# Pooled attention's transposes, its place in the order and the staging's margin: three settings of a fused attention and MLP kernel

## The chip, the cores and the metric

The kernel runs as one program on one core of a Trainium2 chip. The metric is the device time of one execution in microseconds (us). Before the change the median of three timed runs is 923.7 us (923.35 to 924.69).

## What is computed

The reference takes q, k and v of shape (4 batches, 8 heads, 576 tokens, 64). It adds two attentions: one on q, k and v averaged over groups of four tokens (144 pooled tokens, the result repeated four times), and one local attention in which a token sees only tokens less than four away. The sum, 2304 tokens by 512, goes through two feed-forward blocks.

```python
out = np.repeat(sm_attn(q_d, k_d, v_d), 4, axis=2) + local_attn(q, k, v)
x = (x @ w_a) * (x @ w_b) @ w_out          # 512 -> 1536 -> 512
h = x @ w_in                               # 512 -> 2048
out = (h * clip(h + 3, 0, 6) / 6) @ w2_out # 2048 -> 512
```

## The kernel before, in words

**Stages.** Weights arrive as 64-bit words and are decoded on ScalarE (ACT) and VectorE (DVE) into 32-bit values (`decode`, from L246 on). Matmuls of the feed-forward blocks run as three passes over a high and a low part of each operand. Tokens are cut into six blocks of 384. Phase 1 multiplies blocks 0 to 2 with `w_a` and `w_b` (12 column tiles f each); phase 2 does the same for blocks 3 to 5. One *job* (`job`) is one block times one f: two products of 12 matmuls (L625) into two PSUM banks; ACT copies the first (L631), DVE multiplies it by the second (L634), and SP stores it. Then follow `w_out` (L729), `w_in` (L876) and the last product (L1015), each in a scheme that works on sums and differences of weight tiles.

**Attention** runs between the jobs. For each batch there are four *groups* (`pooled`, a pair of heads twice over) and five *units* of up to 116 tokens (`local`). A group does: sums of four tokens on DVE (L385, `dqk`), scores on PE (L395, `dsc`), maximum (L400) on DVE, exponentials on ACT (L409), inverse and scaling on DVE (L415, L416, L337), two transposes on PE (`turn`, L427, four 72x72 matmuls each into a PSUM bank of its own), an ACT copy of each into a `deT` tile (`turned`, L434), the product with v (`pv`, L445) and a copy into `od` (L451). A unit does: scores (L496), mask (L504), maximum (L511, L512), exponentials (L521), inverse and scaling (L527, L528, L337), a transpose (L537), its copy (L541), the product with v (L552), the sum with the pooled result (L565, `xf`) and the split of it into the high part (L573, ACT) and the low part (L578, DVE) of the block's `x`. The jobs of a block read all of its `x`; four batches of 576 tokens make six blocks, so batch 2 fills block 3 with units 0 to 3, and its unit 4 and batch 3's units 0 and 1 fill block 4.

From batch 2 on, the product with v of one item and the scores of the item two further on are one PE step (`both`). The next batch's q and k go into the same four `qk` buffers, and are loaded after the last unit's scores of the batch before have been computed.

**Staging.** 22 tiles of the later weights (6 of `wo`, 8 of `w2i`, 8 of `w2o`) are decoded during phases 1 and 2, combined (L1170 on DVE, L1173 on ACT) and written back to HBM (`staged`). Their decode takes the one `dm` buffer: ACT makes the magnitude (L263), DVE does L277, L278 and L282, ACT L271, then DVE L289.

**What sets the order.** The program's order on every engine is worked out when the kernel is built. A planner (`Plan`) keeps a list of steps, each with an engine, a busy time, a `want` (a priority number, not a time; lowest first), what it follows, and tags that it takes and gives back (`BUFS` and the caps below it say how many of each there are). It walks through modelled time, and gives each free engine the ready step of the lowest want whose tags can be had. A step counts as done for those behind it only after its busy time plus a latency of its engine plus `slack`. On the chip each engine then runs its steps in that fixed order and waits on semaphores. The tag `turn` stands for a transpose on its way to ACT's copy; pooled groups and units share it. `pv` (1) and `m` (3) are such tags for products with v and for jobs; all three also take one of four `b` banks.

Jobs follow each other by 384/332 = 1.157 in want. Batch 2's first unit has t = 25.23; its groups have t - 0.05 + 0.01 g. The job before them has wants 24.29 and 24.79 for its two products, the one before that 23.13 and 23.63. Batch 3's first unit has t = 32.26; batch 2's units 3 and 4 have 28.83 and 31.06. Staged tile i has want 3.6 + 2.4 i. While the queue of PE is short of work before the first job, it is given dummy matmuls (L193, `unread`).

Of the kernel before, what the change touches and what calls it, by code (L numbers as in the profile page):

```python
# [29 lines left out]
HP = 4  # L30
# [8 lines left out]
SOON = 14  # L39
# [116 lines left out]
def fused_kernel(ctx: ExitStack, tc: tile.TileContext, qk, vt, vd, wab, wo, w2i, w2o, mask, out):  # L156
# [4 lines left out]
    F1 = wab.shape[0]  # L161
# [28 lines left out]
    def fill():  # L190
        if not unread:
# [4 lines left out]

    plan = Plan()

    BUFS = {"wh": F1, "raw": 3, "dm": 1, "qk": 4, "vraw": 1, "dqk": 2, "de": 2, "dv": 2, "deT": 2, "od": 2, "e": 2,
            "eT": 2, "xf": 2, "x": 3, "a": 3, "b": 4, "s2": 2, "h0": 3, "X": 6, "y": 8, "w2": 2, "q": 8, "x0": 4, "L": 24,  # L200
            "c": 14}
    plan.cap.update(BUFS)

    plan.cap.update({"turn": 1, "pv": 1, "m": 3})
    plan.loose |= {"dm", "b", "turn", "pv", "m", "s2", "e", "de", "eT", "deT", "xf", "dqk", "a", "q", "y", "c"}

    def slot(pool, shape, dtype, tag, name):
        return pool.tile(shape, dtype, tag=tag, bufs=BUFS[tag], name=name)


    def dve(n):
        return 0.07 + 0.00106 * n

    def dve2(n):
        return 0.1 + 0.00055 * n

    def act(n):
        return 0.1 + 0.00095 * n
# [9 lines left out]
    def ACT(busy, want, run, after=(), take=(), give=(), slack=0.0):  # L228
        return plan.add("ACT", busy, want, run, after, take, give, ACT_L + slack)

    def DVE(busy, want, run, after=(), take=(), give=(), slack=0.0):
        return plan.add("DVE", busy, want, run, after, take, give, DVE_L + slack)
# [3 lines left out]
    def DMA(kb, want, run, after=(), take=(), give=()):  # L236
        i = plan.add("SP", dma(kb), want, run, after, take)
        j = plan.add("-", 0, want, lambda: None, [i], give=give, late=DMA_L)
        issued[j] = i
        return j  # L240
# [5 lines left out]
    def decode(src, want, put, tag, after=(), ahead=4, slack=1.0, raw=None, step=CUT, early=False):  # L246

        T = {}

        def load(a, b):  # L250
            def run():
                if a == 0:
                    T["raw"] = slot(xp if raw == "x" else dp, [P, CUT, W // CUT], mybir.dt.uint64, raw or "raw", "raw")
                nc.sync.dma_start(T["raw"][:, a:b], src[a:b].rearrange("a p c -> p a c"))
            return run

        def words():
            w = T["raw"].rearrange("p a c -> p (a c)").bitcast(U32).rearrange("p (n t) -> p n t", t=2)
            return w[:, :, 0], w[:, :, 1]

        def magnitude():
            T["m"] = slot(dp, [P, W], F32, "dm", "m")
            nc.scalar.activation(T["m"], words()[1].bitcast(F32), AF.Abs)  # L263

        def rounded():

            lo = words()[0]
            if early:
                nc.vector.tensor_scalar(lo, lo, 2.0 ** -29, None, op0=ALU.mult)
            else:  # L270
                nc.scalar.activation(lo, lo, AF.Copy, scale=2.0 ** -29)  # L271

        def exponent():
            m = T["m"]
            mu = m.bitcast(U32)

            nc.vector.tensor_scalar(m, m, W_MIN, W_MAX, op0=ALU.max, op1=ALU.min)  # L277
            nc.vector.tensor_scalar(mu, mu, 3, 0x3FFFFFF8, op0=ALU.logical_shift_left, op1=ALU.bitwise_and)  # L278

        def upper():  # L280
            mu = T["m"].bitcast(U32)
            nc.vector.scalar_tensor_tensor(out=mu, in0=words()[1], scalar=0xC0000000, in1=mu,  # L282
                                           op0=ALU.bitwise_and, op1=ALU.bitwise_or)

        def both():

            lo, hi = words()
            mu = T["m"].bitcast(U32)
            nc.vector.tensor_tensor(mu if put is None else hi, mu, lo, op=ALU.add)  # L289

        def first():
            T["w"] = put()
            nc.scalar.activation(T["w"][:, 0], words()[1].bitcast(F32), AF.Copy)

        def second():
            nc.vector.tensor_tensor(T["w"][:, 1], words()[1].bitcast(F32), T["w"][:, 0], op=ALU.subtract)


        i, loads = None, []
        for a in range(0, CUT, step):  # L300
            i = DMA(256 * step, want - ahead, load(a, a + step), [i and issued[i]], take=[] if a else [raw or "raw"])
            loads.append(i)
        i = loads
        j = ACT(act(W), want, magnitude, i, take=["dm"], slack=slack)
        r = DVE(dve2(W), want, rounded, i) if early else ACT(act(W), want, rounded, i, slack=slack)
        i = DVE(2 * dve2(W), want, exponent, [j])
        i = DVE(dve(W), want, upper, [i])
        i = DVE(dve(W), want, both, [i, r], give=[] if put is None else ["dm"], slack=slack)
        if put is None:
            return i, T  # L310
        i = ACT(act(W), want, first, [i, *after], take=[tag], slack=slack)
        return DVE(dve(W), want, second, [i], give=[raw or "raw"])
# [3 lines left out]
    def unit_tokens(u):  # L316
        return min(UT, S - u % NU * UT)
# [5 lines left out]
    for u in range(B * NU):  # L323
        segs[u], off = [], 0
        while off < unit_tokens(u):
            m, at = divmod(at_token, XT)
# [764 lines left out]
    items = []  # L1091
    for u in segs:
        m = segs[u][0][0]
        i = (segs[u][0][1] + UT - 1) // UT
        t = when[m, 0] - 4 + 0.1 * i if m < 3 else when[m - 3, F1 - 1] - 6 + 1.2 * i
        b = u // NU
        if u % NU == 0:
            items.append([pooled(b, g, t - 0.05 + 0.01 * g, b < 1) for g in range(HP)])
        items[b].append(local(u, t, u < 8 and unit_tokens(u) == UT))

    def alone(part):
        busy, want, run, after, take, give = part
        return PE(busy, want, run, after() if callable(after) else after, take, give)

    def both(one, two):
        def run():
            one[2]()
            two[2]()
        return PE(one[0] + two[0] - 0.33, one[1], run, (one[3]() if callable(one[3]) else one[3]) + two[3], one[4] + two[4], one[5] + two[5])
# [7 lines left out]
    for b, batch in enumerate(items):  # L1117
        behind = []
        for item in batch:
            part = next(item)  # L1120
            if len(behind) < (2 if b >= JOIN else 1):
                i = alone(part)
            elif b >= JOIN:
                before, end = behind.pop(0)
                i = both(end, part)
                close(before, i)
            else:
                before, end = behind.pop(0)
                close(before, alone(end))
                i = alone(part)  # L1130
# [7 lines left out]
    i = plan.add("PE", 0.01, -1000, fill, take=["b", "m"])  # L1138
# [11 lines left out]

    def staged(src, want, dest, right):

        i, T = decode(src, want, None, None, step=1, ahead=4 - SOON)

        def v(n):
            return T["m"].rearrange("p (a c) -> p a c", a=CUT)[:, n]

        def t(n):
            return r7()[:, 3 + n]

        def r7():
            return T["raw"].rearrange("p a c -> p (a c)").bitcast(F32).rearrange("p (a c) -> p a c", c=Q)[:, :7]

        def sums():
            if right:
                ops = ((0, v, 3, v, 0), (1, v, 2, t, 0), (2, v, 2, v, 3), (3, v, 1, t, 1))
            else:
                ops = ((0, v, 3, v, 2), (1, t, 0, v, 0), (2, v, 0, v, 3), (3, v, 1, t, 1))
            for k, (to, f, x, g, y) in enumerate(ops):
                nc.vector.tensor_tensor(t(to), f(x), g(y), op=ALU.subtract if right or k else ALU.add)  # L1170

        def copy():
            nc.scalar.activation(r7()[:, 0:3], T["m"].rearrange("p (a c) -> p a c", a=CUT)[:, 0:3], AF.Copy)  # L1173

        j = ACT(act(3 * Q), want, copy, [i])
        k = DVE(4 * dve(Q), want, sums, [i], slack=0.3)
        plan.add("-", 0, want, lambda: None, [j, k], give=["dm"])
        return [DMA(896, want, lambda: nc.sync.dma_start(dest, r7()), [j, k], give=["raw"])]
# [8 lines left out]
    for i, (name, k) in enumerate(S_["staged"]):  # L1187
        src, dest = {"wo_d": (wo, lambda: wo_d[:, :, k]), "wi_d": (w2i, lambda: wi_d[:, 7 * k:7 * k + 7]),
                     "w_d": (w2o, lambda: w_d[k // CUT][:, :, k % CUT])}[name]
        S_[name, k] = staged(src[k], T1 - LEAD - SOON + PACE * i, dest(), name == "w_d")  # L1190
# [164 lines left out]
```

## Time and profile before

| what | us |
|---|---|
| median of the timed runs | 923.7 |
| the profiled execution's own time | 924.78 |
| its span, first to last instruction | 923.0 |
| PE busy in the span | 909.5 |
| DVE busy | 733.5 |
| ACT busy | 537.1 |

PE is TensorE's matmuls, PEld its weight loads, SP the engine that issues most DMAs. "Busy" adds up instruction spans; "[2.88 <-ACT x L573]" behind an instruction says that its engine was idle for 2.88 us just before it, and that the last thing it waited for was ACT's instruction at line 573 that writes `x`. PEclk is the granted TensorE clock as a share of 2.4 GHz, so 0.50 is the level of 1.2 GHz.

### The profile page before, as it was taken

The numbers are of one execution on the slowest core, as the hardware profiler recorded it, in microseconds if no ns is written. First come the engines' busy times: TensorE is split into PE (matmuls) and PEld (weight loads), VectorE is DVE, ScalarE is ACT, GpSimd is POOL, SyncE is SP. The second block draws the span as 40 slices with busy tenths as digits, with TensorE's granted clock in tenths as the row PEclk, the third lists the DMA queues.
The fourth block names the chain that finished last, engine by engine and source line by source line (L and its number), as shares of the span: only waits on it lengthen the run. The fifth ranks groups of instructions, "written<-read, shape, count | busy, mean of one in ns | idle before, by whom it ended". The sixth has DMA issues, their size and how long they took to land.

```text
span 923.0 us, 18730 instructions
## 1 busy us (share of the span) xinstructions
PE 909.5 (99%) x7076; PEld 876.7 (95%) x7076; DVE 733.5 (79%) x1299; ACT 537.1 (58%) x1234; POOL 3.2 (0%) x40
## 2 busy tenths in 40 slices
PE   9999999999989999999999999999999999999998
PEld 6678899999979999999999999999999999999998
DVE  4999987788978987476977798786566899896983
ACT  3778754547656764452745466666566774554551
POOL 0000000000000000000000000000000000000000
PEclk9999999999989999999999999999999999999999
DMA  9645877566765668888454664634348772707301
GB/s 304 229 131 155 287 229 242 189 211 227 274 238 186 212 207 257 269 265 273 138 167 138 191 190 143 206 112 163 137 172 271 252 242 92 251 2 229 114 18 52
DMA packets 121994, 176.91 MB, mean 192 GB/s; under 512 B 9392, under 2 KB 95664, under 8 KB 121904
## 3 DMA queue, kind: packets, MB, share of 16 engines
q1 hardware_dynamic: 121184, 174.49, 57.4%
q8 instruction: 55, 0.90, 0.4%
q10 hardware_dynamic: 720, 1.23, 0.4%
q14 instruction: 35, 0.29, 0.1%
HBM read 113.03 MB, written 62.65 MB: 190 GB/s over the span
## 4 chain that ended last, share of the span: by engine, by line
PE 92%; DVE 5%; DMA 1%; issue 0%; ACT 0%; POOL 0%; SPq 0%; POOLq 0%; ACTq 0%; DVEq 0%
PE pab L625 32%; PE ph L876 19%; PE oacc L1015 19%; PE acc L729 14%; PE po L552 2%; DMA qk<-qk 1%; PE dsc L395 1%; PE dpo L445 1%; PE oacc L1000 1%; PE sc L496 1%; PE dpt L427 1%; PE unread L193 1%; DVE m L282 1%; DVE dqk L385 1%; PE pt L537 1%; DVE mx L511 0%
## 5 line engine op out<-in xcount | busy, mean ns | idle before, releaser
L625 PE MATMUL pab<-x,wh 128*128 128x384 f32 (+2 forms) x1776 | 323.9, 339 | 3.7 <-ACT x L573 2.9
L625 PEld LDWEIGHTS pab<-x,wh 128*128 128x128 f32 x1776 | 305.2, 190 | 7.3 <-ACT x L573 3.0
L876 PE MATMUL ph<-in,wt 128*128 128x384 f32 x1008 | 175.4, 335 | 0.0
L876 PEld LDWEIGHTS ph<-in,wt 128*128 128x128 f32 x1008 | 175.2, 188 | 0.0
L1015 PE MATMUL oacc<-w2o,in 128*128 128x256 f32 x1440 | 172.4, 283 | 0.0
L1015 PEld LDWEIGHTS oacc<-w2o,in 128*128 128x128 f32 x1440 | 172.4, 191 | 0.0
L729 PE MATMUL acc<-hx,wt 128*128 128x384 f32 x756 | 131.2, 334 | 0.0
L729 PEld LDWEIGHTS acc<-hx,wt 128*128 128x128 f32 x756 | 131.1, 188 | 0.0
L631 ACT ACTIVATE a<-pab 128x384 f32<-128x384 f32 (+2 forms) x74 | 35.6, 482 | 97.3 <-PE pab L625 97.2
L634 DVE TENSOR_TENSOR a<-a,pab 128x384 f32<-128x384 f32 (+2 forms) x74 | 40.0, 541 | 54.6 <-PE pab L625 20.0
L680 ACT ACTIVATE hx<-hr 128x768 fp32r<-128x768 f32 x63 | 52.1, 844 | 40.9 <-PE acc L729 22.3
L683 DVE TENSOR_TENSOR hx<-hr,hx 128x768 fp32r<-128x768 f32 x63 | 58.7, 954 | 18.4 <-ACT hx L680 18.1
L803 ACT ACTIVATE in<-gr 128x384 fp32r<-128x384 f32 x96 | 47.2, 520 | 41.7 <-PE oacc L1015 30.9
L893 DVE TENSOR_TENSOR part<-ph,part 128x384 f32<-128x384 f32 x72 | 39.8, 555 | 31.1 <-PE ph L876 19.9
L901 ACT ACTIVATE r<-part,three 128x384 f32<-128x384 f32 x72 | 43.9, 614 | 26.7 <-DVE part L893 25.7
L806 DVE TENSOR_TENSOR in<-gr,in 128x384 fp32r<-128x384 f32 x96 | 49.6, 550 | 8.1 <-ACT in L803 7.3
L803 ACT ACTIVATE in<-e 128x384 fp32r<-128x384 f32 x72 | 37.3, 525 | 28.8 <-PE oacc L1015 23.7
L885 ACT ACTIVATE part<-ph 128x384 f32<-128x384 f32 x72 | 35.1, 490 | 25.0 <-PE ph L876 24.7
L282 DVE SCALAR_TENSOR_TENSOR m<-raw,m 128x1024 uint32<-128x1024 uint32 x34 | 41.5, 1220 | 0.5
L263 ACT ACTIVATE m<-raw 128x1024 f32<-128x1024 f32 x34 | 38.8, 1141 | 4.0 <-DVE raw L1170 2.0
L904 DVE SCALAR_TENSOR_TENSOR r<-r,part 128x384 f32<-128x384 f32 x72 | 38.9, 549 | 0.9 <-ACT r L901 0.9
L806 DVE TENSOR_TENSOR in<-e,in 128x384 fp32r<-128x384 f32 x72 | 37.8, 551 | 0.8 <-ACT in L803 0.5
(95 smaller groups left out, 1036.6 us busy)
## 6 DMA issues: line engine op xcount, KB each, us to landing
g_d<-r SPq DMA_DIRECT2D x96, 192.0 KB, 2.0
gr<-g_d SPq DMA_DIRECT2D x48, 384.0 KB, 4.2
hr<-h_d SPq DMA_DIRECT2D x72, 192.0 KB, 3.7
h_d<-a SPq DMA_DIRECT2D x70, 192.0 KB, 2.4
raw<-wab SPq DMA_DIRECT2D x12, 1024.0 KB, 8.3
raw<-w2i SPq DMA_DIRECT2D x32, 256.0 KB, 4.0
raw<-w2o SPq DMA_DIRECT2D x32, 256.0 KB, 3.4
wi_d<-raw SPq DMA_DIRECT2D x8, 896.0 KB, 4.4
```

The lines of the kernel that those rows point to most:

```text
L282: nc.vector.scalar_tensor_tensor(out=mu, in0=words()[1], scalar=0xC0000000, in1=mu, op0=ALU.bitwise_and, op1=ALU.bitwise_or)
L625: nc.tensor.matmul(T[k], wab_t[f][:, x, c], xs[n][:, g, y, ja:jb], start=(g == 0 and i == 0), stop=(g == KC - 1 and i == 2))
L634: nc.vector.tensor_tensor(T["a"], T["a"], T[1], op=ALU.mult)
L680: nc.scalar.activation(X[n, kk][:, :, 0], src(), AF.Copy)
L683: nc.vector.tensor_tensor(X[n, kk][:, :, 1], src(), X[n, kk][:, :, 0], op=ALU.subtract)
L729: nc.tensor.matmul(acc[n][e], t[:, x, e * P:(e + 1) * P], X[n, kk][:, j, y], start=(kk == 0 and j == 0 and i == 0 and not onto), stop=(kk ...
L803: nc.scalar.activation(x[0][:, 0], src(), AF.Copy)
L806: nc.vector.tensor_tensor(x[0][:, 1], src(), x[0][:, 0], op=ALU.subtract)
L876: nc.tensor.matmul(acc[k], t[:, x, g * P:(g + 1) * P], X[k, g][0][:, y], start=(g == 0 and n == 0 and not onto), stop=(g == 1 and n == 2), ...
L893: nc.vector.tensor_tensor(s[name], acc[k], s[other], op=ALU.add)
L901: nc.scalar.activation(T["r"], src(), AF.Relu, bias=three)
L1015: nc.tensor.matmul(acc[n][e], X[n, k][0][:, x, e * P:(e + 1) * P], t[:, y], start=(k == 0 and i == 0), stop=(k == K - 1 and i == 2))
```

## The change

Four settings are changed. `deT`, the tiles for transposed pooled weights, go from two to four. The tag `turn` goes from one to two. The groups of batches 2 and 3 get a want 1.5 below their first unit's instead of 0.05; with it move the wants of their loads of q, k (6 below) and v, and of all their steps. The decode inside `staged` is planned with slack 0.0 on the steps that had 1.0 (the magnitude L263, the scaling L271, and L289).

```diff
-    BUFS = {... "dv": 2, "deT": 2, "od": 2, "e": 2,
+    BUFS = {... "dv": 2, "deT": 4, "od": 2, "e": 2,
...
-    plan.cap.update({"turn": 1, "pv": 1, "m": 3})
+    plan.cap.update({"turn": 2, "pv": 1, "m": 3})
...
-            items.append([pooled(b, g, t - 0.05 + 0.01 * g, b < 1) for g in range(HP)])
+            items.append([pooled(b, g, t - (1.5 if b > 1 else 0.05) + 0.01 * g, b < 1) for g in range(HP)])
...
-        i, T = decode(src, want, None, None, step=1, ahead=4 - SOON)
+        i, T = decode(src, want, None, None, step=1, ahead=4 - SOON, slack=0.0)
```

## Rows read from the trace of the kernel before

**Rows 1.** The page: busy time of each engine and its share of the span.

```profile
PE 909.5 (99%) x7076; PEld 876.7 (95%) x7076; DVE 733.5 (79%) x1299; ACT 537.1 (58%) x1234; POOL 3.2 (0%) x40
```

**Rows 2.** Stretches: us, busy (count) of PE, PEld, DVE, ACT, POOL; PEclk, DMA, GB/s.

```profile
20.00:62.50 42.50, 39.36 (x574) 28.94 (x571) 40.99 (x75) 31.91 (x133) 0.00 (x0) 1.00 0.65 215
62.50:124.00 61.50, 60.24 (x689) 53.32 (x686) 59.37 (x107) 46.73 (x154) 0.64 (x8) 1.00 0.66 210
240.00:260.00 20.00, 16.22 (x172) 14.86 (x172) 18.93 (x36) 13.13 (x46) 0.64 (x8) 0.94 0.94 319
260.00:900.00 640.00, 640.00 (x4439) 634.83 (x4439) 505.66 (x890) 370.13 (x723) 0.00 (x0) 1.00 0.56 182
```

**Rows 3.** Who PE waited for: us in total, times, longest.

```profile
PE pab L625 <- ACT x L573: 2.9, 1, 2.9
...
PE pab L625 <- DVE x L578: 0.7, 2, 0.4
```

**Rows 4.** Stretches of 2 us about the long stall.

```profile
256.00:258.00 2.00, 0.43 (x1) 0.28 (x1) 2.00 (x3) 1.72 (x9) 0.00 (x0) 0.87 0.97 318
258.00:260.00 2.00, 1.69 (x5) 1.44 (x5) 1.97 (x6) 2.00 (x10) 0.00 (x0) 0.50 1.05 407
...
264.00:266.00 2.00, 2.00 (x13) 2.00 (x12) 0.48 (x2) 0.00 (x0) 0.00 (x0) 0.93 0.19 75
```

**Rows 5.** The chain that ended last, in order of time: start, us, what.

```profile
124.06 53.20 PE pab L625 x300
...
184.14 6.56 PE pab L625 x36
...
255.38 1.23 DVE m L282
256.61 0.55 DVE xf L565
...
258.56 8.95 PE pab L625 x35
```

**Rows 6.** Timeline of PE, batch 2: start, us, line, tiles, count.

```profile
177.09 0.42 PE L427 MATMUL dpt<-ident,de 72*72 72x72 f32 x4
...
195.39 0.71 PE L445 MATMUL dpo<-deT,dv 72*64 72x144 f32 x8
...
198.89 0.41 PE L427 MATMUL dpt<-ident,de 72*72 72x72 f32 x4
199.10 2.36 PE L625 MATMUL pab<-x,wh 128*128 128x384 f32 x12
201.31 0.41 PE L427 MATMUL dpt<-ident,de 72*72 72x72 f32 x4
...
251.71 0.60 PE L537 MATMUL pt<-ident,e 128*128 128x128 f32 x4
252.91 0.71 PE L395 MATMUL dsc<-dqk 64*72 64x144 f32 x8 [0.59 <-DVE dqk L385]
253.55 1.14 PE L552 MATMUL po<-eT,vz 64*64 64x58 f32 x32
```

**Rows 7.** Timeline of DVE: scaling of batch 2's group 0, and of group 2.

```profile
114.89 0.75 DVE L337 TENSOR_TENSOR de<-de,dz 72x576 f32<-72x576 f32 x1
...
192.14 0.76 DVE L337 TENSOR_TENSOR de<-de,dz 72x576 f32<-72x576 f32 x1
```

**Rows 8.** Line 434 on ACT, the copy of a transpose: duration min/median/max in ns.

```profile
L434 ACT ACTIVATE deT<-dpt x32: 382/406/464, 15.4 to 300.0; 72x288 f32<-72x288 f32 x32
```

**Rows 9.** Stretches: all engines, then tile m's instructions on DVE and ACT.

```profile
204.00:262.00 58.00, 54.22 (x564) 51.25 (x561) 51.62 (x104) 39.61 (x125) 0.64 (x8) 0.96 0.74 253
...
204.00:262.00 58.00, 26.54 (x40) 9.88 (x10) 0.96 0.74 253
```

**Rows 10.** Line 277 on DVE waiting for line 263 on ACT: total, times, longest.

```profile
DVE m L277 <- ACT m L263: 2.9, 3, 1.6
```

**Rows 11.** Line 625 alone, from the stall to unit 1 of batch 3.

```profile
257.50:318.20 60.70, 49.54 (x240) 43.96 (x240) 0.94 0.59 211
```

More of the change, by code (lines that the diff above doesn't have):

```diff
@@ L197, in fused_kernel @@
     plan = Plan()
-    BUFS = {"wh": F1, "raw": 3, "dm": 1, "qk": 4, "vraw": 1, "dqk": 2, "de": 2, "dv": 2, "deT": 2, "od": 2, "e": 2,
+    BUFS = {"wh": F1, "raw": 3, "dm": 1, "qk": 4, "vraw": 1, "dqk": 2, "de": 2, "dv": 2, "deT": 4, "od": 2, "e": 2,
             "eT": 2, "xf": 2, "x": 3, "a": 3, "b": 4, "s2": 2, "h0": 3, "X": 6, "y": 8, "w2": 2, "q": 8, "x0": 4, "L": 24,
```

## The prediction

> **What bounds the kernel now.** I read the page first: PE is busy for 909.5 of 923.0 us [rows 1]. The change takes no matmul of the work away and adds none, so nearly all it can win is PE's 13.5 us without work, and slow clock. The windows say where these are. PE is short by 3.1 us from 20 to 62.5 us, where DVE is busy for 40.99 of 42.50; by 1.3 us from 62.5 to 124; by 3.8 us from 240 to 260; and by nothing in the 640 us from 260 to 900 [rows 2]. The rest lies ahead of 20 us and behind 900. The largest gap is thus one place in batch 2's attention. PE's list of waits names it: 2.88 us for the high part of x (L573), 0.3 of the 0.7 us for its low part (L578), and 0.59 us for the sums of batch 3's first group, 3.8 us together [rows 3, 6]. Phase 1's last job is over by then, and block 3's first job needs the x of batch 2's unit 3.
>
> The gap has a second price. The granted clock falls to half at its end and comes back in the window from 264 us [rows 4]. The 35 matmuls behind the gap took 8.95 us; 36 took 6.56 at full clock, so 35 take 6.38, and 2.6 us were lost [rows 5]. Together 6.4 us. (Upper bound for the idle part: from 251.71 to 258.56, 6.85 us, PE had a transpose, scores, a product with v and one matmul of the job to do, 0.60, 0.71, 1.14 and about 0.18 us, so 4.2 us were lost there, and 6.8 in all; the lower figure uses the rows of idle alone, and I take it, as restarts between small matmuls will stay [rows 5, 6].)
>
> The Trainium skill, page "TensorE: Matmul & The Clock Gate", section Terms, prices such a fall as the throttled time times one minus the granted share. By the windows' clocks (0.87, 0.50, 0.50, 0.50 and 0.93 of 2 us each) that is 3.4 us, an estimate by that page, and the time forecast below would be 0.8 us lower; the matmuls' own count decides here.
>
> **Part 1: groups 1.5 earlier.** Group 0 of batch 2 was scaled at 114.89, and its transpose ran at 177.09 [rows 6, 7]: for 62 us it waited for nothing but its want. So a lower want does start the chain sooner. By how much: want 25.18 lies behind the job with 24.29 and 24.79; want 23.73 lies behind the one with 23.13 and 23.63. That is one whole job, 24 matmuls at 53.20/300 us = 4.3 us [rows 5]. (Taken as a rate, 1.5/1.157 jobs, it would be 5.5 us.) The chain's products, exponentials and DVE steps keep their numbers. Of what is moved with them, the loads of q and k of batch 3 do not move by want: their buffers come free with unit 4's scores, so they come earlier only as the units do. The loads of v, issued by SP one job sooner, pass at most the staging's loads; these have three raw buffers, and no row has PE waiting for them. In return one job runs behind the chain instead of ahead of it, at no cost for PE.
>
> **Part 2: two transposes at once, four deT.** Now a group's two transposes, at 198.89 and 201.31, have 12 matmuls between them [rows 6]. With two turns both go together, and that product drops out of each group's chain: 2.4 us by its row. Group 2 was scaled by 192.90 but transposed at 198.89: it waited until group 1's product (195.39) gave back its two deT tiles [rows 6, 7]. With four it needs not, worth up to 6 us more for the units that follow. Along the four groups that is 2.4 us at the least (the other hops hidden behind DVE) and four times that, 9.6 us, at the most. I take 5, between the one hop and the 6 us of the one wait for deT that a row shows. The second turn holds a second of the four banks for about a copy's length; two banks are left for the products when pv has none. A job alternates between two, so no PE wait is booked; if the cover goes, it is at most one ACT copy, 0.41 us, for each of the 12 groups past batch 0, 5 us [rows 8]; no row has PE waiting for a bank.
>
> **Part 3: staging without slack.** No staged tile is waited for by PE in the trace, so finishing it sooner wins nothing. What it can do is take DVE away. In 204 to 262, tile m's instructions hold DVE for 26.54 us, and DVE is busy for 51.62 of 58 [rows 9]: five tiles at 5.3 us. Being far behind its want, staging outranks attention on DVE. Cost, from below: nothing (the waits are where they are). From above: L277 stood up to 1.6 us for L263 [rows 10], so five tiles stand 8.0 us; and if two of some 11.6 us (58/5) for a tile go, 58/9.6 makes six tiles, one more of 5.3 us. I take 2 us, near the lower end, since L277's three waits were 2.9 us in all, and DVE has 6.4 us to spare in the stretch.
>
> **The sum.** Unit 3's low x came at 258.56 and would have to come 4.2 us earlier for PE not to wait. The chain gains 4.3 + 5 and gives back 2: 7.3 us, enough with 3.1 to spare. So the gap goes: 924.78 - 6.4 = 918.4 for an execution like the profiled one. That stood 1.1 us above the median, so against the median 923.7 - 6.4 = **917.3 us**. Nothing is booked for the first 124 us, where DVE sets the pace; the idle time there is kept for the range.
>
> **What is late next.** Block 4 needs batch 3's unit 1. From the gap to that unit's product PE ran 240 of the 288 matmuls (12 jobs) of block 3 [rows 11]; 48 are left, 8.5 us at 0.177. Batch 3's qk loads come sooner with unit 4's scores and its groups gain by part 2 too, so this cover holds or grows.
>
> **Rivals.**
> *The gap shrinks but stays.* The chain gains only 4.3 + 2.4 and loses 4 on DVE, 2.7 of 4.2: about 1.5 us of idle stays, and the clock holds. 923.7 - 2.3 - 2.6 = 918.8. For it: DVE, which every step of the units passes, is 89% busy there [rows 9].
> *The change doesn't do what it says.* The groups start sooner, but DVE works the units off at the same times, as they are late for it and not for PE; same gap, 923.7, within 1.2. Against it: group 2's wait for deT is no DVE wait.
> *Slower: staging takes DVE.* Place: units 0 to 3 of batch 2. Extra DVE time by the upper bounds is 8.0 + 5.3 = 13.3 us; against the chain's least gain of 6.7 the x of unit 3 comes 6.6 us later, 930.3 us. It decides from the point at which DVE loses more than 6.7 + 1.9 us; 927 in its middle. For it: DVE runs in its fixed order, and the 1.23 us of staging just ahead of xf show whom it lets pass [rows 5]. Against it: 6.4 us of spare DVE time [rows 9]. The Trainium skill ("TensorE: Matmul & The Clock Gate", section on the array's architecture) says that ACT and DVE are strictly first in, first out, which is what this rival needs; the trace agrees so far as the 1.6 us of L277 stand with other work behind it.
>
> **How the numbers follow.** The forecast has 0.60, the shrunk gap 0.10, no effect 0.14, slower 0.16. About 0.2%, 1.9 us, can be told from no change. Faster by more is the forecast and the shrunk gap, 0.70; within it 0.14; slower 0.16. Range: down to 914.0 (6.8 for 6.4, the 1.3 us of idle from 62.5 to 124, and 1.6, half of the 3.1 ahead of it), up to 924.0, which takes in no effect and leaves the slower case out. The likeliest case's own range is 914.0 to 919.
>
> **What would show it.** Right: no wait of PE for x L573 or L578 at block 3's first job; PEclk 1.00 from 240 to 280; L427 in rows of x8; batch 2's first L427 about 4 us before 177; first job of phase 2 about 4 us sooner than 257.57. Part 3 wrong: longer waits of L277 for L263, DVE over 95% in that stretch. The forecast fails if PE has a gap of over 2 us anywhere behind 124 us, or PE waits for L631 or L634, a bank.

## The result and the profile after

The changed kernel takes 912.39 us (median of 4 runs, 911.03 to 913.82) beside 923.83 us for the kernel before: a ratio of 0.9875 [0.9858, 0.9892], 11.4 us less. The forecast was 917.3 us with a range of 914.0 to 924.0, so the sign was right and the gain nearly twice the one forecast, outside the range. The execution profiled below took 913.82 us with a span of 912.0; the one before took 924.78 with 923.0. The difference of the spans, 11.0 us, is what follows.

The page of the changed kernel, busy time of each engine (answers to [rows 1]):

```profile
PE 903.5 (99%) x7058; PEld 872.9 (96%) x7058; DVE 732.5 (80%) x1299; ACT 534.4 (59%) x1234; POOL 3.2 (0%) x40
```

PE has 18 instructions fewer. They are the dummies of L193, 36 where there were 54. Its stretches (columns as in [rows 2]):

```profile
20.00:62.50 42.50, 41.03 (x661) 32.38 (x659) 40.24 (x78) 32.79 (x144) 0.00 (x0) 1.00 0.62 202
62.50:124.00 61.50, 61.50 (x628) 55.96 (x627) 57.96 (x99) 44.24 (x138) 0.64 (x8) 1.00 0.62 205
204.00:262.00 58.00, 57.06 (x543) 53.67 (x542) 53.03 (x107) 37.46 (x121) 0.64 (x8) 1.00 0.80 272
240.00:260.00 20.00, 19.40 (x153) 17.36 (x151) 17.12 (x33) 10.30 (x43) 0.00 (x0) 1.00 0.79 261
260.00:900.00 640.00, 639.17 (x4451) 634.48 (x4451) 506.67 (x893) 369.64 (x710) 0.00 (x0) 1.00 0.56 182
```

PE lost 3.8 us from 204 to 262 before [rows 9] and loses 0.94 now, and the granted clock is 1.00 there. From 20 to 124 us it lost 4.4 [rows 2] and loses 1.47. Who PE waited for (columns as in [rows 3]), and its timeline in batch 2 (as in [rows 6]):

```profile
PE unread L193 <- POOL qk L355: 1.9, 1, 1.9
PE pab L625 <- DVE x L578: 1.2, 2, 1.1
PE acc L729 <- DVE a L634: 0.7, 1, 0.7
PE pab L625 <- ACT x L573: 0.4, 1, 0.4
```

```profile
176.52 0.67 PE L427 MATMUL dpt<-ident,de 72*72 72x72 f32 x8
...
188.88 0.67 PE L427 MATMUL dpt<-ident,de 72*72 72x72 f32 x8
...
197.75 0.71 PE L445 MATMUL dpo<-deT,dv 72*64 72x144 f32 x8
...
246.82 0.44 PE L625 MATMUL pab<-x,wh 128*128 128x384 f32 x1 [0.43 <-ACT x L573]
247.43 2.19 PE L625 MATMUL pab<-x,wh 128*128 128x384 f32 x11 [0.17 <-DVE x L578]
```

The 2.88 us for L573 are 0.43. The transposes go in eights. The last product with v (L445) comes at 197.75, 21.2 us behind the first transpose; before it came at 214.31, 37.2 us behind one at 177.09 [rows 6]. Block 3's first job runs on at 247.43 instead of 258.56 [rows 5], 11.1 us sooner: already the whole gain, and only part of it is the gap.

The rest is from before 124 us. The job's matmuls (L625) alone, up to that time, in the kernel before and in the changed one (us, PE busy and count, PEld busy and count, PEclk, DMA, GB/s):

```profile
0.00:124.00 124.00, 47.33 (x277) 42.30 (x277) 1.00 0.70 225
```

```profile
0.00:124.00 124.00, 53.34 (x318) 49.64 (x319) 1.00 0.67 217
```

41 matmuls more are done, 7.2 us of PE at about 0.175 us each, of which 0.6 goes back, as the kernel before had done one more piece of scores by then. So **6.5 us of lead** stand beside **2.8 us of idle time** at the gap, **2.6 us of slow clock** (the prediction's count from [rows 5]; the fall of [rows 4] is gone), and about 1.1 us from transposes that run as eight in 0.67 instead of twice four in 0.41, in the eight groups of batches 2 and 3. Together 13.0 us. The last matmul of a job comes 12.6 us sooner (419.49 for 432.09): the two pitches told in the last section give 1.0 us and take 1.7. From there on 1.6 us go again, 0.71 of them in the new wait at L729's start, and the span is 11.0 shorter.

### The profile page after: what moved, and what is told of

It reads as the page before. It is cut to its first block, busy times and chain, and to the rows that moved or that the text cites. A ratio compares the mean times of both kernels' runs of the same rounds, so it can differ in the third digit from the quotient of the medians.

```text
span 912.0 us, 18711 instructions
## 1 busy us (share of the span) xinstructions
PE 903.5 (99%) x7058; PEld 872.9 (96%) x7058; DVE 732.5 (80%) x1299; ACT 534.4 (59%) x1234; POOL 3.2 (0%) x40
## 4 chain that ended last, share of the span: by engine, by line
PE 88%; DVE 9%; DMA 1%; issue 1%; ACT 0%; POOL 0%; SPq 0%; DVEq 0%; POOLq 0%
PE pab L625 29%; PE ph L876 19%; PE oacc L1015 18%; PE acc L729 14%; PE dsc L395 2%; PE po L552 1%; PE dpo L445 1%; PE oacc L1000 1%; PE unread L193 1%; DVE raw L1170 1%; DVE m L282 1%; PE sc L496 1%; PE dpt L427 1%; DVE dqk L385 1%; DVE m L289 1%
## 5 line engine op out<-in xcount | busy, mean ns | idle before, releaser
L625 PE MATMUL pab<-x,wh 128*128 128x384 f32 (+2 forms) x1776 | 318.2, 337 | 1.7 <-DVE x L578 1.2
L625 PEld LDWEIGHTS pab<-x,wh 128*128 128x128 f32 x1776 | 303.2, 188 | 4.9 <-DVE x L578 1.8
L729 PE MATMUL acc<-hx,wt 128*128 128x384 f32 x756 | 131.3, 334 | 0.7 <-DVE a L634 0.7
L729 PEld LDWEIGHTS acc<-hx,wt 128*128 128x128 f32 x756 | 131.0, 188 | 1.0 <-DVE a L634 1.0
L631 ACT ACTIVATE a<-pab 128x384 f32<-128x384 f32 (+2 forms) x74 | 35.6, 481 | 79.8 <-PE pab L625 78.4
L634 DVE TENSOR_TENSOR a<-a,pab 128x384 f32<-128x384 f32 (+2 forms) x74 | 39.8, 538 | 46.1 <-PE pab L625 18.3
L803 ACT ACTIVATE in<-e 128x384 fp32r<-128x384 f32 x72 | 37.2, 524 | 28.8 <-PE oacc L1015 23.7
L263 ACT ACTIVATE m<-raw 128x1024 f32<-128x1024 f32 x34 | 38.9, 1144 | 10.9 <-DVE raw L289 4.2
```

The lines of the kernel that those rows point to most:

```text
L625: nc.tensor.matmul(T[k], wab_t[f][:, x, c], xs[n][:, g, y, ja:jb], start=(g == 0 and i == 0), stop=(g == KC - 1 and i == 2))
L634: nc.vector.tensor_tensor(T["a"], T["a"], T[1], op=ALU.mult)
L729: nc.tensor.matmul(acc[n][e], t[:, x, e * P:(e + 1) * P], X[n, kk][:, j, y], start=(kk == 0 and j == 0 and i == 0 and not onto), stop=(kk ...
L803: nc.scalar.activation(x[0][:, 0], src(), AF.Copy)
```

## The experiments

The ratio is always to the kernel before on the same chip in the same series (medians 923.83 to 924.95); differences between kernels of different series are given by the ratios, at 924 us for 1. Brackets hold the 95% interval of a ratio. The letters in the recorded texts stand for the readings that each text spells out. Three questions were open: which edit wins what; whether the early lead is the second turn's; and why leaving slack out of the staging should matter at all. Four `deT` were not run by themselves, nor left out by themselves: what they add is read from experiments 1 and 2 only.

**1. Two turns alone.** `"turn": 1` becomes 2 in the kernel before, nothing else.

> Only turn goes from 1 to 2; deT stays at 2, start and slack as before. Theory A (the groups of batches 0 and 1 wait for each other through the one turn and the two deT, and about 6.6 us of the 11.4 were won ahead of 124 us): with two deT a group still has to wait for the product of the group before it, so about half of the early gain, 3 us by 124 us; the gap at batch 2 shrinks by the hop of 2.4 us but stays above 1 us. 917 to 921 us. Theory B (the early gain is DVE work in another order, the transposes are not what batches 0 and 1 wait for; the gap at batch 2 is all that the change closes): no early gain, 921 to 924 us.

Measured: 921.63 us, 0.9971 [0.996, 0.9982]. 316 matmuls of L625 are done by 124 us, all but two of the lead, and the first job starts at 45.78 instead of 49.63. Yet only 2.7 us are won, since the gap in batch 2 stays. The waits on PE's timeline from 228 to 270 us:

```profile
245.02 1.14 PE L552 MATMUL po<-eT,vz 64*64 64x58 f32 x32 [0.76 <-ACT eT L541]
248.48 0.96 PE L395 MATMUL dsc<-dqk 64*72 64x144 f32 x8 [1.67 <-DVE dqk L385]
250.42 0.69 PE L625 MATMUL pab<-x,wh 128*128 128x384 f32 x1 [0.99 <-ACT x L573]
251.42 6.21 PE L625 MATMUL pab<-x,wh 128*128 128x384 f32 x23 [0.31 <-DVE x L578]
```

3.7 us, as before, although the groups' chain is 25.6 us long (178.90 to 204.50) instead of 37.2: the jobs that cover it came 7 us sooner as well. A further 2.3 us go in four waits of L729, from 425 to 439 us.

**2. Two turns and four deT**, `"turn": 2, "deT": 4`.

> turn 2 and deT 4; start and slack as before. Theory A: the full early gain, 60 + 258 = 318 of line 625's matmuls by 124 us as in the changed kernel (277 before), and the gap at batch 2 at least halved by the shorter chain of its groups: 912 to 917 us. Theory B: 277 to 285 matmuls by 124 us, the gap closed or halved: 917.5 to 921 us.

914.82 us, 0.9893 [0.9873, 0.9912]. The gap is gone without an earlier start, and the chain is 21.2 us long as in the changed kernel. But there is a new wait, of L625 for ACT's copy of an earlier job (L631):

```profile
358.80 8.74 PE L625 MATMUL pab<-x,wh 128*128 128x384 f32 x48 [0.46 <-ACT a L631]
...
368.71 4.42 PE L625 MATMUL pab<-x,wh 128*128 128x384 f32 x24 [1.17 <-ACT a L631]
...
375.21 4.97 PE L625 MATMUL pab<-x,wh 128*128 128x384 f32 x18 [2.08 <-ACT a L631]
```

3.7 us. ACT itself stood there until a job's store (`h_d<-a`) gave its buffer back; SP issued that store behind loads for the staging and for `w_out`. Even so the two further `deT` are worth 0.78% on top of the second turn, 7.2 us: without them (experiment 1) the gap and the waits of L729 eat the lead.

**3. The start alone**, `t - 0.05` becomes `t - (1.5 if b > 1 else 0.05)`.

> Only the groups of batches 2 and 3 go 1.5 earlier. Both theories: 277 matmuls of line 625 by 124 us as before. Theory A (one job, 4.3 us, against the 4.2 needed): the gap all but closes and the clock does not fall, 917.5 to 919.5 us. Theory C (DVE, not the start, sets when batch 2's units end): the gap stays above 2.5 us and the clock falls, 922 to 924 us.

918.28 us, 0.9932 [0.9918, 0.9947]. The first transpose comes at 174.04 for 177.09, 3.1 us sooner. Ahead of it stand 552 of L625's matmuls for 576, which is the one job that Part 1 reckoned with; this execution's first 16 dummies took 6.44 us for 5.10, so from a like start it is 4.4 us. The gap and the fall of the clock are gone, and the early lead isn't there (276 matmuls). The 0.68% are 6.3 us: what gap and clock were worth in the kernel before, where the forecast had 6.4.

**4. The slack alone**, `slack=0.0` in `staged`.

> Only the staging is planned with slack 0. Theory A (staging has no part in the gain and takes at most 2 us of DVE's time in batch 2): 277 matmuls by 124 us, the gap the same or up to 2 us longer, 923 to 926 us. Theory D (staged tiles out of the way sooner free DVE for batch 2): the gap shrinks by 2 us or more, 918 to 921 us.

919.79 us, 0.9951 [0.9934, 0.9967]. No early lead (276), and again no gap, with the groups starting at 178.38, no sooner than before, and ending after 35.1 us. DVE from 204 to 262 us does more, not less:

```profile
204.00:262.00 58.00, 58.00 (x628) 54.42 (x626) 55.33 (x109) 40.58 (x128) 0.64 (x8) 1.00 0.76 269
```

DVE is busy 95% of the stretch, beside 51.62 us [rows 9], and PE all of it. Staging has no part in the 3.7 us more: tile m's instructions hold DVE for 26.69 us, beside 26.54. L277 does wait longer for L263 over the whole span, 7.0 us beside 2.9 [rows 10], but unit 3's sum (L565) comes at 250.99 instead of 256.53. Staging's last store goes out at 381.1 us instead of 421.0.

**5. All but the slack**: the changed kernel with the staging's slack put back.

> The changed kernel with the staging's slack back at 1.0. Theory F (with turn and deT, PE runs ahead of the staging in phase 2, stores of jobs and staging jam on SP's queue, and slack 0 is what takes this away): PE waits 2 us or more for L631 between 340 and 420 us as in the run of turn and deT, 913.5 to 916 us. Theory G (slack 0 adds nothing once the gap at batch 2 is closed): no such wait, 911.5 to 913 us.

919.78 us, 0.9936 [0.992, 0.9952]: 0.61% or 5.6 us worse than the changed kernel, with the early lead (320) and without the gap. The time goes at the end of phase 2. PE on its timeline, SP on its own, and then the chain that ended last (start, us, what):

```profile
434.07 0.69 PE L729 MATMUL acc<-hx,wt 128*128 128x384 f32 x1 [4.33 <-ACT hx L680]
```

```profile
421.68 0.52 SPq L1178 DMA_DIRECT2D w_d<-raw  x1
422.29 1.83 SPq L1225 DMA_DIRECT2D wt<-wi_d  x2
427.08 1.76 SPq L671 DMA_DIRECT2D hr<-h_d  x4
```

```profile
421.20 0.43 DVE raw L1170
...
421.68 0.52 SPq L1178
...
422.95 6.99 DMA wt<-wi_d
...
429.96 1.06 ACT wt L1230
...
432.19 0.96 DVE hr L700
...
433.17 0.85 ACT hx L680
```

Phase 2's last job matmul is issued at 418.0 here, but the staging goes on: DVE combines its last tile at 421.20, and its store goes out on SP at 421.68. Behind it on SP stand the loads of the next weights (`wi_d`, 7.0 us), and behind these four loads of `hr`, the operand of `w_out`. They go into a `raw` buffer (L667), and SP stood until the store had landed and given one back (total, times, longest):

```profile
SPq L671 <- DMA w_d<-raw: 2.9, 1, 2.9
```

ACT and DVE convert the weights ahead of the subtraction L700, ACT makes `hx`, and PE has stood 4.33 us. The loads of `hr`, issued from 427.08 with 4.8 us to landing, would have come at about the same time; the rows don't part the two. The clock then falls (0.80 over 434 to 450 us): PE does 72 matmuls of L729 there in 15.62 us, and 94 in 16.00 in the changed kernel. In the changed kernel the staging's last store goes out at 398.69, and the loads of `hr` that come before the next weights are all out by 418.6. In the kernel before phase 2 ends at 432.1 and the staging's last store goes out at 421.0: a margin of 11 us, and nobody waits. The faster attention uses this margin up, and the slack's edit gives it back. It is not the slack alone that sets where the staging ends: in experiment 2, which has the old slack too but not the earlier start, the last store goes out at 408.35, and L729 doesn't wait.

**6. All but the start.**

> The changed kernel with the groups' want back at 0.05 below their units. Theory F: turn and deT already close the gap at batch 2 and slack 0 keeps the end of phase 2 free of waits, so next to nothing is lost: 911 to 913.5 us, no wait for L631. Theory G (the earlier start is needed beside turn and deT): gap or waits of 1.5 us or more come back, 914 to 917 us.

914.89 us, 0.9882 [0.9866, 0.9898]. The gap is back in part, and L631 is waited for twice (1.6 us):

```profile
245.67 0.44 PE L625 MATMUL pab<-x,wh 128*128 128x384 f32 x1 [1.86 <-ACT x L573]
246.67 7.92 PE L625 MATMUL pab<-x,wh 128*128 128x384 f32 x35 [0.56 <-DVE x L578]
```

The interval overlaps that of the changed kernel: once the chain is short, the runs don't set the earlier start apart from nothing (0.07%).

**7. All but the second turn**: the changed kernel with `"turn": 1`.

> The changed kernel with one turn (four deT, groups 1.5 earlier, no slack). Theory H: no early lead (272 to 285 matmuls of L625 by 124 us, first job at 49 to 50 us), no gap of PE over 0.7 us at block 3's first job, clock 1.00 there: 916 to 919 us. The forecast's own reckoning (the second turn is needed to close the gap): a gap of 1 us or more stays. Rival (early lead comes from the order as a whole, not from the turn): over 300 matmuls by 124 us and at most 914 us.

920.45 us, 0.9949 [0.9932, 0.9967], slower than the text's main reading had it. 296 matmuls by 124 us, between its two guesses: batch 0's last product with v (L445) comes at 33.64 for 35.17, though the first job is no sooner (50.40). That points to the four deT, which no run has alone. With that lead and a chain of 31.9 us the gap is back, which supports the forecast's view that the second turn is needed once the jobs come sooner:

```profile
250.34 0.63 PE L537 MATMUL pt<-ident,e 128*128 128x128 f32 x4 [1.61 <-ACT e L521]
251.65 1.14 PE L552 MATMUL po<-eT,vz 64*64 64x58 f32 x32 [0.69 <-ACT eT L541]
254.86 0.44 PE L625 MATMUL pab<-x,wh 128*128 128x384 f32 x1 [1.42 <-ACT x L573]
256.00 5.84 PE L625 MATMUL pab<-x,wh 128*128 128x384 f32 x23 [0.70 <-DVE x L578]
```

**8 and 9. Two turns for one early batch only.** In the kernel before, the groups and units of batch 0 (or of batch 1) take a tag of two places, all others the old one.

```diff
-    plan.cap.update({"turn": 1, "pv": 1, "m": 3})
+    plan.cap.update({"turn": 1, "turn0": 2, "pv": 1, "m": 3})
...
-        t = [PE(0.3, want, turn(c), [i], take=["b", "turn", "deT"], ...
+        t = [PE(0.3, want, turn(c), [i], take=["b", "turn0" if b == 0 else "turn", "deT"], ...
```

> The kernel before, with two turns for batch 0 only (deT 2, one turn for batches 1 to 3). Theory A (the early gain is batch 0's: its groups' transposes in pairs bring the first units, and with them the first job, forward): first job 3.5 us or more before the 49.6 of before, 305 or more of line 625's matmuls by 124 us (277 before, 316 with turn alone). Theory A2 (batch 1's groups share it): about 295. The total may be anything from 917 to 923 us, by whether the gap at batch 2 stays.

926.04 us, 1.001 [0.9995, 1.0025], no gain. The first job does start at 46.37, 3.3 us sooner, but only 281 matmuls are done by 124 us. Two waits for decoded weights (L296, the last step of their decode), which the kernel before has not, take 3.0 us of it back, and the granted clock is 0.97 from 62.5 to 124 us where it was 1.00:

```profile
79.25 3.91 PE L625 MATMUL pab<-x,wh 128*128 128x384 f32 x12 [1.91 <-DVE wh L296]
...
92.33 2.32 PE L625 MATMUL pab<-x,wh 128*128 128x384 f32 x12 [1.09 <-DVE wh L296]
```

> The kernel before with two turns for batch 1 only (batch 0, 2 and 3 keep one). Theory H (the lead of the first 124 us is won in both batches, and batch 0's part is only worth something if batch 1 hands it on): first job still at 49 to 50 us, 290 to 305 matmuls of L625 by 124 us, gap at 258 us stays, 920.5 to 924 us. Rival (it is all batch 1's; batch 0's earlier product with v is hidden anyway): 310 or more matmuls by 124 us and 917 to 920 us. Rival (the two-turn order pays only from the first batch on): at most 285 matmuls, 923 to 926 us.

924.58 us, 1.0001 [0.9992, 1.0011], no gain either: 286 matmuls by 124 us, the first job at 49.87, and the gap larger, 4.13 us for L573. So batch 0 alone is worth 4 matmuls, batch 1 alone 9, both together 39 (experiment 1). The lead is neither's alone. That much is shown; that it is the common order of decoding and attention on DVE that couples them is read from the waits, and wasn't tried by itself.

**10. No dummies**: the kernel before without its filler, `plan.filler = ...` left out.

> The kernel before without the dummy matmuls of line 193 after the first (the planner's filler is left out; the result is not affected). Theory A (the chain of transposes, copies and products of batch 0 sets the first job; the dummies only fill PE's waits): 273 to 281 matmuls of line 625 by 124 us, and if the clock falls ahead of 60 us it costs at most 2 us: 923 to 926 us. Theory E (the dummies, up to four at a time between two transposes, are what delays the chain, and turn 2 gains by having 18 fewer of them): first job 3 us or more sooner, 918 to 921 us.

929.13 us, 1.0045 [1.0029, 1.0061]. One way to read the lead was that fewer dummies stand in the chain's way. Nothing here bears it out: with only the first dummy left, the first job starts later (53.1 for 49.63) and fewer jobs' matmuls are done by 124 us (258). But the run doesn't exclude it at full clock, as the granted clock is low in it. The windows of this kernel:

```profile
20.00:40.00 20.00, 17.39 (x262) 14.38 (x259) 19.07 (x35) 12.62 (x55) 0.00 (x0) 0.70 0.79 272
40.00:60.00 20.00, 17.31 (x202) 13.15 (x198) 15.61 (x28) 16.26 (x65) 0.00 (x0) 0.79 0.38 116
```

**11 and 12. A better version?** The changed kernel with its groups 2.7 ahead instead of 1.5, and the changed kernel with slack 0.5.

> The changed kernel with its groups of batches 2 and 3 2.7 ahead of their units instead of 1.5. The idle time of 0.94 us that is left at block 3's first job goes: 911 to 912.5 us, not to be told from the changed kernel. Rival (one job more behind the chain only changes the order elsewhere, as leaving out the slack's setting did): a new wait of PE of 2 us or more at phase 2's end or for a bank, 914 to 919 us. Rival (DVE, not the start, sets unit 3's time by now): the same 0.9 us of idle, the same time.

914.05 us, 0.9885 [0.9864, 0.9905]; not to be told from the changed kernel. No wait is left at block 3's first job, from 204 to 262 us PE is busy for all 58.00, but L625 waits for L631 at 345.91 and 352.37 (0.38 and 1.95 us), as in experiment 2.

> The changed kernel with slack 0.5 in the staging's decode instead of 0.0. If the slack works by how early the staging ends (398.7 us in the changed kernel, 421.7 with slack 1.0), then half of it ends between 405 and 412 us, and the wait of L729 for ACT's hx at 434 us is gone or under 1 us: 912 to 915 us. If it works by the order that it happens to give, the time may lie anywhere from 911 to 920 us with no relation to where the staging ends.

912.33 us, 0.9862 [0.9837, 0.9888], the same as the changed kernel. The staging ends at 400.8, not at 405 to 412, and L729 doesn't wait; L625 waits 1.8 us for L631. The slack's effect isn't graded in the way the text supposed, and half of it is as good as none. No version beats the change.

## Why the prediction was wrong

**The step that failed: "Nothing is booked for the first 124 us, where DVE sets the pace".** This left out 6.5 us. The view was right, DVE was busy for 40.99 of 42.50 us [rows 2]; the reading of it was not. DVE is as full after (40.24), and the first job starts 6.7 us sooner with one matmul (42.92 for 49.63) and runs on from 44.46. It takes the first two units' 232 tokens, so it needs the low part of the second unit's x (L578), and that comes 5.5 us sooner. Before and after:

```profile
49.29 0.64 DVE L578 TENSOR_TENSOR x<-po,x 128x464 fp32r<-128x464 f32 x1
49.63 1.84 PE L625 MATMUL pab<-x,wh 128*128 128x232 f32 x12
```

```profile
43.77 0.63 DVE L578 TENSOR_TENSOR x<-po,x 128x464 fp32r<-128x464 f32 x1
44.46 1.49 PE L625 MATMUL pab<-x,wh 128*128 128x232 f32 x11 [1.08 <-DVE x L578]
```

What differs is what DVE does ahead of that instruction. Two of the steps that decode phase 1's weights, from the start of the span to its end (49.93 before, 44.40 after):

```profile
L289 DVE CUSTOM_DVE_ANT_0 raw<-raw,m 128x2048 uint16<-128x2048 uint16 x3 | 3.7, 1219 | 0.0
L269 DVE TENSOR_SCALAR raw<-raw 128x1024 uint32<-128x1024 uint32 x4 | 2.7, 684 | 0.0
```

```profile
L289 DVE CUSTOM_DVE_ANT_0 raw<-raw,m 128x2048 uint16<-128x2048 uint16 x2 | 2.4, 1221 | 0.0
L269 DVE TENSOR_SCALAR raw<-raw 128x1024 uint32<-128x1024 uint32 x2 | 1.4, 688 | 0.0
```

DVE was full because the order let it decode further weight tiles while the groups stood in the queue for the one turn. The products with v of batch 0's four groups came at 18.65, 23.63, 28.84 and 35.17; with two turns and four deT, at 19.16, 22.82, 26.98 and 30.85. The steps are 5.0 to 6.3 us before and 3.7 to 4.2 after, so it was the hand-over of the transposes, PE to ACT and back, that set the pace, the very hop that Part 2 took out for batch 2. The forecast booked Part 2 for batches 2 and 3 alone. Experiment 1 shows that the second turn by itself brings the lead, experiment 8 that batch 0's turn sets when the first job starts.

The first step of the prediction hid this too: PE's 13.5 us without work are not "nearly all it can win", as the 909.5 us of busy PE hold the dummies, which the planner adds only where PE has nothing else. One row of the kernel before:

```profile
40.86 1.89 PE L193 MATMUL unread<-ident 128*128 128x512 bf16 x8
```

PE's next instruction starts at 42.59, so a dummy holds PE for 0.216 us, and the 30 of them between 20 and 62.5 us took 6.5 us beside the 3.1 us of idle time. After the change 18 fewer run, 3.9 us. With 2.9 us less idle time from 20 to 124 us and 1.1 us less for the transposes of batches 0 and 1 (6.9 and 5.8 us), and less 1.3 us because the first 16 dummies took 6.39 us in this execution and 5.10 before, that is 6.6 us: the lead, counted a second way.

The Trainium skill ("Perfetto Trace Analysis", section Identifying the Most-Contended Engine) tells the bottleneck among VectorE, ScalarE and GpSimd by occupancy. These rows differ: DVE's is 96% before and 95% after (40.99 and 40.24 of 42.50), and the first job starts sooner all the same, with no work of DVE made faster.

**Part 2's size.** "I take 5", between 2.4 and 9.6 us, was too small, and its upper end too. The chain of batch 2's groups shrank by 11.6 us with the second turn alone (experiment 1: 25.6 for 37.2) and by 4.4 more with four deT (experiment 2: 21.2), 16.0 in all. All four groups lost their hop on the path (3.2, 2.4, 2.4 and 2.4 us between the two transposes of a group); none was hidden behind DVE. Of these 16 us only what the gap needed turned into time, which is why the error cost little there. What the gap needed was not the 4.2 us of the sum either: the jobs that cover the chain come sooner by the early lead as well, and with two turns alone the gap stayed although the chain was 11.6 us shorter.

**Part 3, "No staged tile is waited for by PE, so finishing it sooner wins nothing".** It is wrong twice. The slack alone wins 0.5%, 4.5 us (experiment 4), as DVE works the stretch off with fewer holes; the 2 us that it was to cost measured as 0.15 us more of tile m on DVE. Why the new order has fewer holes was not tried. And without it the changed kernel gives back 0.6% (experiment 5), as the staging's end then lies behind phase 2's, and its last store holds the buffer that `w_out`'s operand is to be loaded into. No wait of the kernel before showed that, because there the margin was 11 us. The test named for this part, DVE over 95% in that stretch, points the wrong way: experiment 4 has it, with PE at 58.00 of 58.

**What was right.** The gap closes but for 0.94 us, of which 0.43 and 0.17 us are still waits for x (L573 and L578) at block 3's first job; the clock stays at 1.00, the transposes go in eights, no job waits for a bank, and block 4 found its x in time. L729 does wait 0.71 us for L634, which the prediction had named as a sign of failing. Gap and clock were worth 6.3 us (experiment 3) where 6.4 were booked, 5.4 of it in the changed kernel, in which the 0.94 us are left. Part 1's one job of lead is there to the matmul in experiment 3, 4.4 us from a like start. In the changed kernel batch 2's first L427 comes at 176.52 and not 4 us before 177, as 612 of L625's matmuls stand ahead of it where 576 did. The slower rival, staging taking DVE from the units, did not come: with the slack alone units 1 and 3 had their sums 6.2 and 5.5 us sooner. The Trainium skill ("TensorE: Matmul & The Clock Gate", section on the array's architecture) has DVE strictly first in, first out. The longer waits of L277 in experiment 4 (7.0 us for 2.9) agree with it so far as other work stood behind them. The rival needed more than that, that the units wait as well, and the runs don't show it.

Where each edit's worth lies: alone, the second turn wins 0.3%, the start 0.7%, the slack 0.5%; left out of the whole, they cost about 0.7%, 0.1% and 0.6%. Four deT add 0.8% to the second turn. The gains don't add, as the start, the slack and the shorter chain each close the same gap, and the second turn wins its lead only where the other two keep the gap and the end of phase 2 from eating it.

## What to carry to other kernels

A full engine is not yet the one that sets the pace: ask which of its instructions the late result needs, and whether the others could have come later; where a hand-over is taken out of a routine, look for every stage that runs this routine, the start of the kernel first. Before booking an edit at nothing because no one waits for its result, measure the margin (here 11 us between the staging's end and the phase that reuses its buffers) and ask whether the rest of the change will use it up. In an order planned ahead, each edit shifts the next bottleneck, so test parts by leaving one out of the whole as well as by adding one to the kernel before.

## What the hardware showed that was not expected

The same matmul of a job, 128x128 by 384 columns at full clock and with PE never idle, runs at one of two pitches (time from one start to the next) that hold for hundreds of instructions. Rows of the chain that ended last, in order of time (start, us, what), in the kernel before (beside the first row of [rows 5], 53.20 us for 300, 177.3 ns each):

```profile
344.86 87.56 PE pab L625 x504
```

and in the changed kernel:

```profile
112.55 52.20 PE pab L625 x300
...
328.48 87.13 PE pab L625 x492
```

That is 173.7 ns late in the kernel before, and 174.0 early and 177.1 late in the changed one: the two have changed places. Some 3.4 ns on 492 matmuls are 1.7 us that the changed kernel loses in phase 2, and 1.0 us that it wins on the 300. The start alone and the slack alone keep the order of the kernel before (48.96 us for 276, then 87.57 for 504, with the start); two turns alone swap it (60.53 for 348, then 85.01 for 480). But two turns for batch 1 alone gives the short pitch in both stretches (58.44 for 336, 85.48 for 492), and two turns for batch 0 alone the long one in both (55.31 for 312, 91.36 for 516). So all four pairs occur, no edit goes with one pitch, and the cause stays open.
